# Pairs instead of groups of four in a feed-forward backward, and a changed order of the first loads

## Chip, core and metric

The kernel runs on one core of a Trainium2 chip. The metric is the time of one execution on the device in microseconds (us). Five runs of the kernel before gave 637.66 to 637.92 us, with a median of 637.72 us.

## What is computed

A sequence of 2048 tokens of width 640 goes through two blocks that a gate mixes. All of it is bf16; the kernel returns the output and six gradients.

```python
def _A_ref(x, wqkv, wo):                     # linear attention, 32 heads of 20
    phi = lambda t: jnp.where(t > 0, t + 1, jnp.exp(t)) + 1e-6
    pq, pk = phi(q), phi(k)
    kv = jnp.einsum("bhsd,bhse->bhde", pk, v)
    z = jnp.einsum("bhsd->bhd", pk)
    num = jnp.einsum("bhqd,bhde->bhqe", pq, kv)
    den = jnp.einsum("bhqd,bhd->bhq", pq, z)[..., None] + 1e-6
    ...
def _B_ref(x, w1, w2):                       # feed-forward, 640 -> 1728 -> 640
    h = jnp.maximum(jnp.einsum("bsd,df->bsf", x, w1), 0)
    return jnp.einsum("bsf,fd->bsd", h, w2)

g = sigmoid((x * gate_w).sum(-1, keepdims=True))
out = g * _A_ref(x, A_wqkv, A_wo) + (1 - g) * _B_ref(x, B_w1, B_w2)
# returned: out, and the gradients of x, wqkv, wo, w1, w2, gate_w for a given grad_out
```

## The kernel before

**Tiles and stages.** The tokens are cut into 16 tiles of 128 (`NT`), and the tiles into 4 groups of 4 (`NG`, `G`). The width 640 is 5 chunks of 128 (`KD`); the inner width 1728 is 13 chunks of 128 and a rest of 64, so 14 chunks (`KF`). The stages follow each other on TensorE: the keys of all tiles (`k_part`), the state of the attention (`yp`), queries and forward feed-forward per tile, the gradient of w2, the backward of the attention, **the backward of the feed-forward** (`fb_a`, `fb_b`), the gradient of w1 (`dw1_half`) with the gradient of the keys (`dk_chunk`), the gradients of wqkv, and the gradient of x.

**The start.** `x` and the key weights come in by DMAs that SyncE (SP) and ScalarE (ACT) issue. ACT issues the gate row `gst` (line 408) and then three chunks of the key weights (line 406); SP issues x tiles 0, 1 and 2, weight chunks 3 and 4, and x tiles 3 and 4 (line 334). TensorE needs x transposed. The first `NPE` = 5 tiles are transposed by TensorE itself (`xt`, lines 446 and 449) into PSUM, and DVE and ACT copy them to SBUF (lines 347, 346, 451, 452). The other tiles come transposed by DMA (line 325): one for tiles 5 to 7, one for 8 to 11, one for 12 to 15 (`XLD`). The first of these waits for the matmul `k_part(1, [2])`. The order of TensorE's instructions in this part is written by hand (lines 477 to 502): warm-up matmuls on a constant (line 461) stand before and between the first transposes, and `k_part(i, ks)` adds the products of the weight chunks `ks` to the key tile `kp` of token tile `i`. Behind it, ACT takes an exponential of the finished key tile (line 394) and DVE two steps (396, 397), which also free its PSUM buffer.

**PSUM.** All stages share one tag of four PSUM buffers, each of two banks.

**The backward of the feed-forward.** `fb_a(i, half)` multiplies grad_out with w2 (line 818, 10 matmuls of 2 x 432 columns per half), ACT scales the product (822), DVE applies the mask of the ReLU (824, 825), and behind the second half SP issues a DMA transpose of the tile to a ring of 6 buffers `hTb` (line 325). `fb_b(i)` multiplies the transposed tile with w1, 13 chunks by 26 matmuls (line 341). The rest of 64 rows uses half the rows of the array; `tail_pair` (lines 578 to 583) runs the rests of two tiles side by side, one on rows 0 to 63 (line 582) and one on rows 64 to 127 (line 583). Before the change four tiles form a group: `fb_b` of the two even tiles comes first, then `fb_tails` runs both pairs' rests one behind the other, then the odd tiles. `step(i)` sets what stands between: the two `fb_a` of tile `i`, small products (`small_0` to `small_3`) that use some of the same buffers, and behind tile 15 the first four `dw1_half`. `step` runs four tiles ahead of `fb_b`.

**Order and places.** Outside of the hand-written part a scheduler orders the instructions of each engine. Nearly all of SBUF is one tile, `arena`; a planner (`_Arena.plan`) gives each buffer a place from its size and its planned times, so that buffers with other times can share a place. A load into a place waits for the last reader of what was there.

Of the kernel before, what the change touches and what calls it, by code (L numbers as in the profile page):

```python
# [81 lines left out]
def kernel(  # L82
# [34 lines left out]
    def ring(name, elems, count, t0, t1):  # L117
        ar.add(name, elems * count * B2, t0, t1)
        rings[name] = [elems, count, 0]
# [46 lines left out]
    ar.add("dKVT", KD * D * B2, T_FB + 40, T_FB + 65)  # L166
    ar.add("Q", KD * D * B2, T_FB + 58, T_DWK - 10)
    ar.add("N", KD * D * B2, T_DWK, T_END)
    ring("hTb", KF * P, 6, T_FB, T_DW1 + 5)
    ring("wst", D, 4, T_FB + 88, T_FB + 112)  # L170
    ar.add("dwoT", KD * D * B2, T_FB + 15, T_FB + 52)
    ar.add("dwo", KD * D * B2, T_FB + 45, T_FB + 80)
    ring("dxst", 2 * D, 2, T_FB + 5, T_DW1 + 5)
    ar.add("xN2", NT * D * B2, T_DW1 - 25, T_DX + 5)
    for g in range(NG):
        ar.add(f"xS{g}", G * P * KD * B2, T_DW1, T_DWK - 10)
        ar.add(f"dk{g}", G * D * B2, T_DW1 + 5 + 15 * g, T_DX)
        ar.add(f"dkT{g}", G * D * B2, T_DW1 + 5 + 15 * g, T_END)
    ring("pkr", 2 * D, 3, T_DW1 - 20, T_DWK)
# [31 lines left out]

    xN = aview("xN", NT * DQX, i=NT)
    xN2 = aview("xN2", NT * D, i=NT)
    NPE = 5
    XLD = [(NPE, 2 * G)] + [(g * G, (g + 1) * G) for g in range(2, NG)]

    def xT_view(a, b):
# [109 lines left out]
    def after(late, early, wait=False):  # L327

        tc.add_manual_dep(late.ins, early.ins.name, mybir.DependencyInfo(
            mybir.DependencyClass.Sync if wait else mybir.DependencyClass.NoSync,  # L330
            mybir.DependencyReason.DATA), reason="order of loads")
# [71 lines left out]
        return load_N(xN[:, a:b, 0:D], x2[a * P:b * P, :])  # L403

    def wk_load(eng, k):
        eng.dma_start(wk_s[:, k, 0:D], A_wqkv[k * P:(k + 1) * P, D:2 * D])

    nc.scalar.dma_start(gst[:], gate_w.rearrange("(k p) -> k p", p=P))
    x_load(0, 1)
    wk_load(nc.scalar, 0)  # L410
    x_load(1, 2)
    wk_load(nc.scalar, 1)
    x_load(2, 3)
    wk_load(nc.scalar, 2)
    wk_load(nc.sync, 3)
    wk_load(nc.sync, 4)
    for i in range(3, NPE):
# [19 lines left out]
    def xt(i):  # L437
        if i < 3:
            tp = flat(pp("xtp"))[:, 0:D].rearrange("p (k s) -> p k s", k=KD)
        else:  # L440
            if i == 3:
                kps["x"] = psp.tile([P, 2, 1024], BF16, tag="PP", bufs=4, name="xtp2")
            tp = kps["x"][:, i - 3, 0:D].rearrange("p (k s) -> p k s", k=KD)
        for k in range(KD):
            if i < 3:
                nc.tensor.matmul(tp[:, k, :], lhsT=xN[:, i, csl(k)], rhs=ident[:], start=True, stop=True,
                                 skip_group_check=True)
            else:
                nc.tensor.transpose(tp[:, k, :], xN[:, i, csl(k)], ident[:])
        if i in (1, 2):  # L450
            nc.vector.tensor_copy(xTv[i][0][:, 0:2, :], tp[:, 0:2, :])
            nc.scalar.copy(xTv[i][0][:, 2:KD, :], tp[:, 2:KD, :])
        else:
            copy_out(0 if i == 4 else 1, xTv[i][0], tp)
# [4 lines left out]
    def warm_up(n, cols=512):  # L459
        for _ in range(n):  # L460
            nc.tensor.matmul(wp_[:, 0, 0:cols], lhsT=warm[:, 0:P], rhs=warm[:, 0:cols], start=True, stop=True)

    def k_part(i, ks):
        if 0 in ks:
            kps[i] = pp("kp")
        kp, last = kps[i], 3 if i < 3 else KD - 1
        for k in ks:
            mm = mm_cols(kp, xT(i, k), lambda a, e: wk_s[:, k, a:e], k == 0, k == last, spl=DSP1)
        if last in ks:
            nc.scalar.activation(rg_t[:, i:i + 1], flat(kp)[:, D:D + 1], ACT.Exp, scale=-1.0)  # L470
            phi_chain(flat(kp)[:, 0:D], pkN[:, i, :])
            if i % 4 == 3:
                nc.sync.dma_start(pk_d[(i - 3) * P:(i + 1) * P, :].rearrange("(i p) d -> p i d", p=P),
                                  pkN[:, i - 3:i + 1, :])
        return mm

    wp_ = pp("warm")
    with tc.manual_schedule(engines={mybir.EngineType.PE}):
        warm_up(4)
        warm_up(1, 256)  # L480
        xt(0)
        tp = psp.tile([P, KD, P], BF16, tag="PP", bufs=4, name="gwtp")
        nc.tensor.transpose(tp[:, 0, 0:KD], gst[:], ident[0:KD, 0:KD])
        nc.vector.tensor_copy(wk_s[:, :, D:D + 1], tp[:, 0, 0:KD].unsqueeze(2))
        warm_up(3)
        k_part(0, [0])
        xt(1)
        xt(2)
        k_part(1, [0])
        k_part(0, [1])  # L490
        k_part(1, [1])
        k_part(2, [0, 1])
        k_part(0, [2])
        after(xT_ld[0], k_part(1, [2]), wait=True)
        k_part(2, [2])
        k_part(0, [4, 3])
        xt(3)
        k_part(1, [4, 3])
        xt(4)
        k_part(2, [4, 3])  # L500
        k_part(3, range(KD))
        k_part(4, range(KD))
    for i in range(NT):
        if i >= NPE:
            k_part(i, range(KD))
# [323 lines left out]
            load_T(dhTs[i], hs(i))  # L829

    def fb_b(i):

        if i % 2 == 0:
            ops[i] = pp("dp")
        dp, dT = ops[i], dhTs[i]
        for kf in range(KF - 1):
            mm_cols(dp, dT[:, kf, :], lambda a, e: w1T_s[:, kf, a:e], i % 2 == 0 and kf == 0,
                    i % 2 == 1 and kf == KF - 2)
        if i % 2 == 1:
            fb_out(i)  # L840

    def fb_tails(i):

        for t in (i, i + 2):
            ops[t + 1] = pp("dp")
            tail_pair(ops[t], ops[t + 1], dhTs[t][:, KF - 1, :], dhTs[t + 1][:, KF - 1, :], w1T_s[:, KF - 1, :], True)
        fb_out(i)
        fb_out(i + 2)

    def fb_out(i):  # L850
        pr, ii = i // 2, i % 2
        dhTs.pop(i)
        if ii == 0:
            dx_st[pr] = rnext("dxst").rearrange("p (i d) -> p i d", i=2)
        nc.scalar.copy(dx_st[pr][:, ii, :], flat(ops.pop(i))[:, 0:D])
        if ii == 1:
            nc.scalar.dma_start(rows2(dxB_d, pr), dx_st.pop(pr))

# [19 lines left out]
    def small_3(ts):  # L878
        for t in ts:
            ps = pp("dwv")  # L880
            win_mms(ps, lambda j: YT_s[:, j, csl(t)], dKV_s)
            st = rnext("wst")
            copy_out(t + 1, halves(st), ps[:, :, 0:HD])
            nc.scalar.dma_start(out_2[csl(t), 2 * D:3 * D], st)


# [24 lines left out]
    def dw1_half(n):  # L911
# [8 lines left out]
        nc.scalar.copy(st.rearrange("p (b c) -> p b c", b=2), wp[:, :, 0:NBW])  # L920
        nc.scalar.dma_start(out_4[csl(m), 2 * half * NBW:(2 * half + 2) * NBW], st)

    smalls = {3: small_0, 7: small_2, 12: small_3}

    def step(i):
        if i >= NT:
            dw1_half(i - NT)
            if i == NT:
                for g in range(NG):
                    load_T(xSg[g], x2[g * G * P:(g + 1) * G * P, :])  # L930
                pk_load(0)
                pk_load(1)
            return
        fb_a(i, 0)
        if i in (0, 1):
            dz_add(NT - 2 + i)
        if i == 1:
            for m in range(KD):
                load_T(XT_s[:, :, csl(m)], X_s[:, m, :])
        if i == 2:  # L940
            load_T(woT_s, A_wo)
        if i == 4:
            nc.sync.dma_start(dwoT_d.rearrange("(k p) d -> p k d", p=P), dwoT_s)
        if i == 5:
            load_T(wvT_s, A_wqkv[:, 2 * D:3 * D])
        if i == 6:
            nc.sync.dma_start(dKVT_d.rearrange("(k p) d -> p k d", p=P), dKVT_s)
            load_T(dwo_s, dwoT_d)
        if i == 8:
            nc.sync.dma_start(Q_d.rearrange("(k p) d -> p k d", p=P), Q_s)  # L950
            nc.sync.dma_start(out_3.rearrange("(i p) d -> p i d", p=P), dwo_s)
            nc.sync.dma_start(YT_s, YT_d.rearrange("(k p) d -> p k d", p=P))
        if i == 10:
            load_T(dKV_s, dKVT_d)
        if i in smalls:
            smalls[i](range(0, 2))
        fb_a(i, 1)
        if i in smalls:
            smalls[i](range(2, KD))
        if i == NT - 3:  # L960
            for g in range(NG):
                load_N(xN2[:, g * G:(g + 1) * G, :], x2[g * G * P:(g + 1) * G * P, :])

    for i in range(G):
        step(i)
    for i in range(0, NT, G):
        step(i + G)
        fb_b(i)
        step(i + G + 1)
        fb_b(i + 2)  # L970
        fb_tails(i)
        fb_b(i + 1)
        if i == 0:
            small_1()
        step(i + G + 2)
        fb_b(i + 3)
        step(i + G + 3)
    dk_chunk(0)
    dk_chunk(1)
    done = 2  # L980
    for n in range(G, 2 * KD):
        dw1_half(n)
        while done < NT and done < n * 2 + 1:
            dk_chunk(done)
            done += 1
        if n == 8:
            for g in range(NG):
                load_N(dqN[:, g * G:(g + 1) * G, 0:D], dq_d[g * G * P:(g + 1) * G * P, :])
            nc.vector.tensor_copy(dqN[:, :, D:D + 1], dl_t[:].unsqueeze(2))
# [91 lines left out]
```

## Time and profile before

| what | value |
|---|---|
| median of 5 runs | 637.72 us |
| the profiled execution's own time | 637.66 us |
| its span from first to last instruction | 635.9 us |
| TensorE (PE) matmuls busy | 627.1 us, 99% |
| VectorE (DVE), ScalarE (ACT), GpSimd (POOL) busy | 269.8, 147.7, 97.8 us |
| start of the backward of the feed-forward | 319.48 us |
| first matmul of the gradient of w1 | 429.50 us |
| granted TensorE clock | 1.00 |

The profiled execution lies 0.06 us under the median; 1.8 us of it lie outside of the span. PE is busy nearly all the time, so a change counts if it alters PE's own work or makes PE wait. Matmuls overlap: a row's duration is longer than the distance to the next one, and the distance is what adds up.

### The profile page before, as it was taken

Reading aid. Unit: us, or ns where it says so; the run is one execution under the profiler, and the core shown is the slowest. Engines: PE = TensorE matmul, PEld = TensorE weight load, DVE = VectorE, ACT = ScalarE, POOL = GpSimd, SP = SyncE. Lnnn points to the kernel's source line nnn. Section 1 sums busy time; section 2 is a strip of 40 time slices with the busy share of each in tenths; the row PEclk is TensorE's granted clock in tenths of the full one; section 3 lists DMA queues with packets and bytes.
Section 4 is the critical chain, followed back from the end, with each engine's and each line's share of the span. In section 5 each row is a group of like instructions: output and inputs, shape, how many; then the busy total and the mean of one; then the engine's idle time right before and its main releaser. Section 6 shows DMA issues by size and latency. Waiting matters only on the chain.

```text
span 635.9 us, 10499 instructions
## 1 busy us (share of the span) xinstructions
PE 627.1 (99%) x4406; PEld 352.2 (55%) x4482; DVE 269.8 (42%) x523; ACT 147.7 (23%) x208; POOL 97.8 (15%) x95
## 2 busy tenths in 40 slices
PE   8999999999999999999999999999999999999998
PEld 4555555555555555555555555555555555555554
DVE  4832864454444145555994241510016340004442
ACT  4513321122221123222153343331210011110000
POOL 0050742453334022322001000000000000000000
PEclk9999999999999999999999999999999999999999
DMA  7999996544554793942799998955137659991111
GB/s 177 315 395 206 192 248 148 121 92 84 129 120 97 194 198 100 211 135 73 168 190 219 260 256 178 240 136 126 49 117 180 172 109 230 242 258 42 42 42 43
DMA packets 228473, 103.93 MB, mean 163 GB/s; under 512 B 185098, under 2 KB 227722, under 8 KB 228426
## 3 DMA queue, kind: packets, MB, share of 16 engines
q1 hardware_dynamic: 217344, 90.48, 60.9%
q10 hardware_dynamic: 11082, 12.79, 6.2%
q8 instruction: 35, 0.57, 0.4%
q14 instruction: 12, 0.10, 0.0%
HBM read 28.43 MB, written 28.84 MB: 90 GB/s over the span
## 4 chain that ended last, share of the span: by engine, by line
PE 98%; issue 1%; ACT 1%; DVE 0%
PE op L341 12%; PE dxp L341 10%; PE hp L565 9%; PE gp L818 9%; PE w1p L917 9%; PE dp L341 9%; PE w2p L341 9%; PE yp L341 3%; PE xp L341 3%; PE rp L341 3%; PE wkp L341 3%; PE dkp L341 3%; PE qp L341 3%; PE kp L341 3%; PE wqp L1014 3%; PE wqp L1015 1%
## 5 line engine op out<-in xcount | busy, mean ns | idle before, releaser
L341 PEld LDWEIGHTS <-arena 128*128 128x128 bf16 x2978 | 230.6, 98 | 179.6 <-issue 2.1
L341 PE MATMUL op<-arena 128*128 128x128 bf16 (+1 forms) x567 | 79.1, 298 | 0.5
L565 PE MATMUL hp<-arena 128*128 128x432 bf16 x320 | 62.6, 346 | 0.0
L341 PE MATMUL dxp<-arena 128*128 128x128 bf16 (+1 forms) x441 | 60.8, 297 | 0.5
L818 PE MATMUL gp<-arena 128*128 128x432 bf16 x320 | 60.9, 346 | 0.2
L917 PE MATMUL w1p<-arena 128*128 128x432 bf16 x320 | 60.0, 346 | 0.0
L341 PE MATMUL dp<-arena 128*128 128x128 bf16 (+1 forms) x402 | 58.3, 296 | 0.9
L341 PE MATMUL w2p<-arena 128*128 128x128 bf16 (+1 forms) x408 | 58.5, 297 | 0.4
L917 PEld LDWEIGHTS <-arena 128*128 128x128 bf16 x320 | 30.9, 98 | 26.6
L818 PEld LDWEIGHTS <-arena 128*128 128x128 bf16 x320 | 30.7, 98 | 26.2 <-issue 0.5
L565 PEld LDWEIGHTS <-arena 128*128 128x128 bf16 x320 | 30.0, 98 | 26.7 <-issue 1.8
L822 ACT ACTIVATE tb<-gp,omg_t 128x864 bf16<-128x864 f32 x32 | 31.4, 980 | 40.9 <-PE gp L818 39.2
L825 DVE TENSOR_TENSOR arena<-tb,tb 128x864 bf16<-128x864 bf16 x32 | 19.4, 606 | 48.8 <-ACT tb L822 48.2
L901 DVE TENSOR_TENSOR tb<-dkp,dzb 128x640 bf16<-128x640 f32 x16 | 13.1, 820 | 59.2 <-PE dkp L341 59.2
L604 DVE SCALAR_TENSOR_TENSOR tb<-op,arena 128x640 bf16<-128x640 f32 x16 | 13.1, 821 | 47.7 <-ACT arena L602 47.7
L528 POOL TENSOR_TENSOR f<-tb,zb 128x640 f32<-128x640 bf16 x16 | 23.3, 1457 | 60.4 <-DVE tb L397 49.6
L711 POOL TENSOR_TENSOR f<-zb,grd 128x640 f32<-128x640 bf16 x16 | 20.3, 1270 | 75.2 <-DVE grd L709 75.2
L602 ACT CAST arena<-op 128x640 bf16<-128x640 f32 x16 | 11.1, 692 | 81.8 <-PE op L341 47.2
L1038 DVE TENSOR_TENSOR arena<-dxp,f 128x640 bf16<-128x640 f32 x15 | 12.4, 825 | 36.7 <-PE dxp L341 36.7
L920 ACT CAST arena<-w1p 128x864 bf16<-128x864 f32 x10 | 8.8, 878 | 75.2 <-PE w1p L917 75.2
L542 POOL TENSOR_TENSOR arena<-tb,grd 128x640 bf16<-128x640 bf16 x16 | 20.3, 1269 | 30.0 <-DVE grd L536 23.5
L341 PE MATMUL rp<-arena 128*128 128x128 bf16 (+1 forms) x157 | 24.2, 297 | 0.2
(121 smaller groups left out, 609.5 us busy)
## 6 DMA issues: line engine op xcount, KB each, us to landing
out_dram<-arena ACTq DMA_DIRECT2D x28, 160.0 KB, 3.7
arena<-in_A_x_dram SPq DMA_DIRECT2D x6, 640.0 KB, 5.1
pk_d<-arena SPq DMA_DIRECT2D x4, 640.0 KB, 9.7
arena<-in_grad_out_dram SPq DMA_DIRECT2D x4, 640.0 KB, 4.6
e_d<-arena SPq DMA_DIRECT2D x8, 320.0 KB, 2.8
out_dram<-arena ACTq DMA_DIRECT2D x8, 320.0 KB, 2.3
arena<-e_d SPq DMA_DIRECT2D x8, 320.0 KB, 3.6
dq_d<-arena SPq DMA_DIRECT2D x8, 320.0 KB, 3.5
```

Of the source, the lines that this page charges most:

```text
L341: mm = nc.tensor.matmul(ps_tile[:, b, 0:e - a], lhsT=lhsT, rhs=rhs_fn(a, e), start=start, stop=stop, **kw)
L528: return nc.gpsimd.tensor_tensor(tzs[i][:], pqs[i][:], zb[:], ALU.mult)
L542: nc.gpsimd.tensor_tensor(heads(pg), heads(pq[:]), hb(grd[:]), ALU.mult)
L565: nc.tensor.matmul(hp[:, nb, 0:NBW], lhsT=xT(i, k), rhs=w1_s[:, k, blk * NBW:(blk + 1) * NBW], start=(k == 0), stop=(k == KD - 1))
L604: nc.vector.scalar_tensor_tensor(jk[:], flat(op)[:, 0:D], 1.0, doX(i)[:, 0:D], ALU.mult, ALU.mult, accum_out=T_t[:, i:i + 1])
L711: nc.gpsimd.tensor_tensor(heads(wz[:]), heads(zb[:]), hb(w32[:]), ALU.mult)
L818: nc.tensor.matmul(gp[:, nb, 0:NBW], lhsT=doTg[i // G][:, k, gsl(i)], rhs=w2T_s[:, k, blk * NBW:(blk + 1) * NBW], start=(k == 0), stop=(k ...
L822: nc.scalar.activation(gs[:], gp[:, :, 0:NBW], ACT.Copy, scale=omg_t[:, i:i + 1])
L825: nc.vector.tensor_tensor(hs(i)[:, rng], msk[:], gs[:].rearrange("p b c -> p (b c)"), ALU.mult)
L901: nc.vector.tensor_tensor(a_[:], flat(kp)[:, 0:D], dzb[:], ALU.add)
L917: nc.tensor.matmul(wp[:, nb, 0:NBW], lhsT=xN2[:, i, csl(m)], rhs=hs(i)[:, blk * NBW:(blk + 1) * NBW], start=(i == 0), stop=(i == NT - 1))
L1014: nc.tensor.matmul(wp[:, 0, :], lhsT=lhsT, rhs=dqN[:, i, 0:512], start=(i == 0), stop=(i == NT - 1))
```

## The change

There are two parts.

At the start, the first chunk of the key weights is issued ahead of the gate row on ACT, and one of three warm-up matmuls behind the first transpose goes; the gate row's transpose moves behind the other two. `NPE` falls from 5 to 4: x tile 4 is neither loaded for TensorE's transpose nor transposed by it, and the first DMA transpose brings tiles 4 to 7. It waits for `k_part(0, [1])`, which stands five key steps earlier than `k_part(1, [2])`.

In the backward of the feed-forward, the groups of four become pairs: `tail_pair` runs once per pair, directly behind `fb_b` of its even tile. `fb_a` still runs four tiles ahead (`LAGB`); the halves of `fb_a` stand both ahead of `fb_b` for even tiles and on its two sides for odd ones. The ring `hTb` has 5 buffers, the transposed x for `dk_chunk` (`xS`) is planned 25 us earlier and its loads stand ahead of the last tile, and `small_3` copies with ACT alone where it took turns with DVE. The planner gives most buffers another place.

```diff
-    ring("hTb", KF * P, 6, T_FB, T_DW1 + 5)
+    ring("hTb", KF * P, 5, T_FB, T_DW1 + 5)
...
-        ar.add(f"xS{g}", G * P * KD * B2, T_DW1, T_DWK - 10)
+        ar.add(f"xS{g}", G * P * KD * B2, T_DW1 - 25, T_DWK - 10)
...
-    NPE = 5
+    NPE = 4
...
-    nc.scalar.dma_start(gst[:], gate_w.rearrange("(k p) -> k p", p=P))
     x_load(0, 1)
-    wk_load(nc.scalar, 0)
+    gst_ld = nc.scalar.dma_start(gst[:], gate_w.rearrange("(k p) -> k p", p=P))
+    after(gst_ld, wk_load(nc.scalar, 0))
     x_load(1, 2)
-    wk_load(nc.scalar, 1)
+    after(wk_load(nc.scalar, 1), gst_ld)
...
         xt(0)
+        warm_up(2)
         tp = psp.tile([P, KD, P], BF16, tag="PP", bufs=4, name="gwtp")
         nc.tensor.transpose(tp[:, 0, 0:KD], gst[:], ident[0:KD, 0:KD])
         nc.vector.tensor_copy(wk_s[:, :, D:D + 1], tp[:, 0, 0:KD].unsqueeze(2))
-        warm_up(3)
         k_part(0, [0])
         xt(1)
         xt(2)
         k_part(1, [0])
-        k_part(0, [1])
+        after(xT_ld[0], k_part(0, [1]), wait=True)
         k_part(1, [1])
         k_part(2, [0, 1])
         k_part(0, [2])
-        after(xT_ld[0], k_part(1, [2]), wait=True)
+        k_part(1, [2])
         k_part(2, [2])
         k_part(0, [4, 3])
         xt(3)
         k_part(1, [4, 3])
-        xt(4)
         k_part(2, [4, 3])
         k_part(3, range(KD))
-        k_part(4, range(KD))
...
     def fb_b(i):
-
-        if i % 2 == 0:
+        pr, ii = i // 2, i % 2
+        dT = dhTs.pop(i)
+        if ii == 0:
             ops[i] = pp("dp")
-        dp, dT = ops[i], dhTs[i]
+        dp = ops.pop(i)
         for kf in range(KF - 1):
...
         if ii == 0:
+            ops[i + 1] = pp("dp")
+            tail_pair(dp, ops[i + 1], dT[:, KF - 1, :], dhTs[i + 1][:, KF - 1, :], w1T_s[:, KF - 1, :], True)
             dx_st[pr] = rnext("dxst").rearrange("p (i d) -> p i d", i=2)
-        nc.scalar.copy(dx_st[pr][:, ii, :], flat(ops.pop(i))[:, 0:D])
+        nc.scalar.copy(dx_st[pr][:, ii, :], flat(dp)[:, 0:D])
...
-            copy_out(t + 1, halves(st), ps[:, :, 0:HD])
+            nc.scalar.copy(halves(st), ps[:, :, 0:HD])
...
-    for i in range(0, NT, G):
-        step(i + G)
-        fb_b(i)
-        step(i + G + 1)
-        fb_b(i + 2)
-        fb_tails(i)
-        fb_b(i + 1)
-        if i == 0:
-            small_1()
-        step(i + G + 2)
-        fb_b(i + 3)
-        step(i + G + 3)
+    for i in range(NT + LAGB):
+        if i < NT:
+            fb_a(i, 0)
...
+            if i % 2 == 0 or i == NT - 1:
+                fb_a(i, 1)
+        else:
             dw1_half(i - NT)
+        if i >= LAGB:
+            fb_b(i - LAGB)
+        if i < NT - 1 and i % 2 == 1:
+            fb_a(i, 1)
...
+        if i == NT - 2:
+            for g in range(NG):
+                load_T(xSg[g], x2[g * G * P:(g + 1) * G * P, :])
+            pk_load(0)
+            pk_load(1)
```

More of the change, by code (lines that the diff above doesn't have):

```diff
@@ L405, in wk_load @@
     def wk_load(eng, k):
-        eng.dma_start(wk_s[:, k, 0:D], A_wqkv[k * P:(k + 1) * P, D:2 * D])
-    nc.scalar.dma_start(gst[:], gate_w.rearrange("(k p) -> k p", p=P))
+        return eng.dma_start(wk_s[:, k, 0:D], A_wqkv[k * P:(k + 1) * P, D:2 * D])
     x_load(0, 1)
-    wk_load(nc.scalar, 0)
+    gst_ld = nc.scalar.dma_start(gst[:], gate_w.rearrange("(k p) -> k p", p=P))
+    after(gst_ld, wk_load(nc.scalar, 0))
     x_load(1, 2)
-    wk_load(nc.scalar, 1)
+    after(wk_load(nc.scalar, 1), gst_ld)
     x_load(2, 3)
-    wk_load(nc.scalar, 2)
+    after(wk_load(nc.scalar, 2), gst_ld)
     wk_load(nc.sync, 3)
@@ L831, in fb_b @@
     def fb_b(i):
-        if i % 2 == 0:
+        pr, ii = i // 2, i % 2
+        dT = dhTs.pop(i)
+        if ii == 0:
             ops[i] = pp("dp")
-        dp, dT = ops[i], dhTs[i]
+        dp = ops.pop(i)
         for kf in range(KF - 1):
[L837 to L852, printed above, removed]
+            mm_cols(dp, dT[:, kf, :], lambda a, e: w1T_s[:, kf, a:e], ii == 0 and kf == 0, ii == 1 and kf == KF - 2)
         if ii == 0:
+            ops[i + 1] = pp("dp")
+            tail_pair(dp, ops[i + 1], dT[:, KF - 1, :], dhTs[i + 1][:, KF - 1, :], w1T_s[:, KF - 1, :], True)
             dx_st[pr] = rnext("dxst").rearrange("p (i d) -> p i d", i=2)
-        nc.scalar.copy(dx_st[pr][:, ii, :], flat(ops.pop(i))[:, 0:D])
+        nc.scalar.copy(dx_st[pr][:, ii, :], flat(dp)[:, 0:D])
         if ii == 1:
@@ L921, in dw1_half @@
         nc.scalar.dma_start(out_4[csl(m), 2 * half * NBW:(2 * half + 2) * NBW], st)
+    LAGB = 4
     smalls = {3: small_0, 7: small_2, 12: small_3}
-    def step(i):
-        if i >= NT:
-            dw1_half(i - NT)
[L928 to L943, printed above, removed]
-        if i == 5:
[L945 to L957, printed above, removed]
@@ new lines @@
+    for i in range(NT + LAGB):
+        if i < NT:
+            fb_a(i, 0)
+            if i in (0, 1):
+                dz_add(NT - 2 + i)
+            if i == 1:
+                for m in range(KD):
+                    load_T(XT_s[:, :, csl(m)], X_s[:, m, :])
+            if i == 2:
+                load_T(woT_s, A_wo)
+            if i == 5:
+                load_T(wvT_s, A_wqkv[:, 2 * D:3 * D])
+            if i == 4:
+                nc.sync.dma_start(dwoT_d.rearrange("(k p) d -> p k d", p=P), dwoT_s)
+            if i == 6:
+                nc.sync.dma_start(dKVT_d.rearrange("(k p) d -> p k d", p=P), dKVT_s)
+                load_T(dwo_s, dwoT_d)
+            if i == 8:
+                nc.sync.dma_start(Q_d.rearrange("(k p) d -> p k d", p=P), Q_s)
+                nc.sync.dma_start(out_3.rearrange("(i p) d -> p i d", p=P), dwo_s)
+                nc.sync.dma_start(YT_s, YT_d.rearrange("(k p) d -> p k d", p=P))
+            if i == 10:
+                load_T(dKV_s, dKVT_d)
+            if i in smalls:
+                smalls[i](range(0, 2))
+            if i % 2 == 0 or i == NT - 1:
+                fb_a(i, 1)
+        else:
+            dw1_half(i - NT)
+        if i >= LAGB:
+            fb_b(i - LAGB)
+        if i < NT - 1 and i % 2 == 1:
+            fb_a(i, 1)
+        if i == 5:
+            small_1()
@@ L962, in step @@
                 load_N(xN2[:, g * G:(g + 1) * G, :], x2[g * G * P:(g + 1) * G * P, :])
-    for i in range(G):
-        step(i)
-    for i in range(0, NT, G):
-        step(i + G)
-        fb_b(i)
-        step(i + G + 1)
-        fb_b(i + 2)
-        fb_tails(i)
-        fb_b(i + 1)
-        if i == 0:
-            small_1()
-        step(i + G + 2)
-        fb_b(i + 3)
-        step(i + G + 3)
+        if i == NT - 2:
[3 more added lines that the diff above has]
+            pk_load(1)
     dk_chunk(0)
@@ L980 @@
     done = 2
-    for n in range(G, 2 * KD):
+    for n in range(LAGB, 2 * KD):
         dw1_half(n)
```

## The prediction

> **What bounds the kernel now.** I read the page first: its busy times, then the list of what PE waited for, then PE's timeline in the two places that the change touches. Engine, busy time, share of the span:
>
> ```profile
> PE 627.1 (99%) x4406; PEld 352.2 (55%) x4482; DVE 269.8 (42%) x523; ACT 147.7 (23%) x208; POOL 97.8 (15%) x95
> ```
>
> PE has no idle time to give back except a few tenths. The list of its waits (who, for whom, us in total) has three lines:
>
> ```profile
> PE warm L461 <- DVE arena L401: 1.3, 1, 1.3
> PE kp L341 <- DVE arena L451: 0.2, 1, 0.2
> PE kp L341 <- DVE arena L397: 0.2, 1, 0.2
> ```
>
> All are in the first 12 us. So in the backward stage only PE's own steps and new waits count, and at the start the chain to the first keys. The chain of waits at the start (start, us, what):
>
> ```profile
> 5.40 0.53 PE kp L341 x2
> 5.93 0.50 PE xtp L446 x5
> 6.43 0.02 issue
> 6.46 0.44 DVE arena L451
> 6.89 0.05 issue
> 6.94 2.91 PE kp L341 x20
> ...
> 10.05 0.60 ACT tb L394
> ...
> 11.04 0.84 DVE arena L397
> ```
>
> The reader sees that PE goes on at 6.94 when DVE has copied x tile 1, and that tile 3's keys (11.92) wait for the PSUM buffer of tile 0's, through ACT and DVE. The PE timeline around one group of rests (start, us, line, output, shape):
>
> ```profile
> 350.08 0.22 PE L341 MATMUL dp<-arena 128*128 128x128 bf16 x1
> 350.23 0.39 PE L582 MATMUL dp<-arena 64*128 64x512 bf16 x1
> ...
> 350.73 0.22 PE L582 MATMUL dp<-arena 64*128 64x128 bf16 x1
> ...
> 350.88 0.39 PE L341 MATMUL dp<-arena 128*128 128x512 bf16 x1
> ```
>
> Two pairs' rests run here in one piece. Entering it takes 0.15 us from start to start, leaving it 0.15, where a 128-column step between full-array matmuls takes 0.055 (five on line 449 take 0.44 with the last one's 0.22).
>
> Last, DMA transposes of x, each alone in its window of the DMA view; the last number is us from issue to landing:
>
> ```profile
> arena<-in_A_x_dram SPq DMA_TRANSPOSE x1, 4.8
> arena<-in_A_x_dram SPq DMA_TRANSPOSE x1, 7.1
> arena<-in_A_x_dram SPq DMA_TRANSPOSE x1, 5.5
> ```
>
> They are tiles 5 to 7 (issued 9.05), tiles 8 to 11 behind it (10.72), and four tiles on an empty queue (410.34).
>
> **The backward stage.** The matmuls are the same in number and shape: 13 chunks per tile, four half-row matmuls per pair. What changes is how often PE goes into half rows and back. One piece costs 2 x (0.15 - 0.055) = 0.19 us. Before there are 4 such pieces, after 8: **+0.76 us**. The forward pass has the pair form already: at 98.02 to 98.55 the same two distances of 0.15 stand around one pair, so the price does not depend on the group's length. PE is the bound on both sides of each piece, so nothing hides it.
>
> *Buffers.* With pairs at most two `dp` buffers are held, with the group of four up to four. The stage shows no PE wait for `dp` before, so nothing is won. Three waits of 0.29 stand where the small products end (335.43, 368.17, 403.16): three of them take 1.1 us of PE and the next tile needs a buffer that ACT empties in 0.98 after its own 0.2 delay. The first two stay as they are. At the third, ACT now takes all copies: behind the pair's rests it empties `dp` (0.69) and then the products (0.69 each). The last product waits for the first of these (free about 1.0 after the rests, PE there at 0.85: 0.15), the next `gp` for the second (free 1.7, PE there at 1.57: 0.13). Sum 0.28 against 0.29: **0**, between -0.2 (the old turns) and +0.7 (one more copy in the row).
>
> *Transposed tiles.* A tile's transpose is issued behind ACT and DVE (0.98 + 0.61 + 0.18) and lands 4 to 7 us later. The rests of a pair need the odd tile six `gp` blocks of 1.83 and two `fb_b` of 3.5 after it was made, 18 us; before it was four blocks and two `fb_b`, 14 us. A slot of the ring of 5 is free when `fb_b` of the tile five earlier is done, which is behind. The x loads for the keys' gradient now stand between these transposes on SP and hold it 3.5 us each (410.34: 3.48); SP's longest issue here, 8.5 us at 361.57, still fits in 18 - 2 - 7 = 9. **0**; without that cover a late tile costs what exceeds 9 us.
>
> *Places.* Loads wait for other readers now. The closest case I find is the transpose of w1's last chunk, which now stands ahead of the last forward transpose on SP: it issues in 1.3 us, where that tile landed 2.9 us ahead of its use. **0**, up to +0.3.
>
> **The start.** One warm-up less is 0.43 us of PE at half speed (4.76 to 5.19). The first key matmul then waits for DVE's copy of x tile 0 (3.93 + 0.82 = 4.75), and starts at about 4.85 instead of 5.19; with the gate row's transpose now in line, 0.29 of this is left at the next transposes, and DVE's copy and the step at 6.94 move by the same **-0.29**. Against it: x tile 0 is issued at 0.80 and lands at 2.90, just in time for 3.15; weight chunk 0 now is issued at the same moment, not 0.6 later. Its 160 KB take 0.47 us at the 340 GB/s that the DMAs move there (3 to 7 us), so tile 0 lands 0 to 0.47 later, of which 0.1 is free. That gives -0.29 to +0.08; I take half sharing, **-0.1**. The gate row stands behind the chunk, which needs no more than the 3.3 us it took before: it is there at 4.2, needed at 4.6. The earlier first chunk itself gives nothing: it landed at 4.65 and was used at 5.19.
>
> Matmul distances double before about 6.2 us (0.107 against 0.056 for 128 columns), 4.95 us after the first matmul at 1.25. The Trainium skill (TensorE: Matmul & The Clock Gate, "What's actually happening") gives about 3.4 us of sustained work and a free-running window, and says that the moment varies; five runs within 0.26 us speak against a large variation here. By its rule a gap within the window could move the opening to the next window, and half of 3.4 us would be lost: the sum would be +2.4 instead of +0.7. It speaks against the change; no row shows such a miss.
>
> *Tile 4.* Let K be the step at 6.94. Before, tile 5 starts at 14.66 = K + 7.71. PE loses the two parts of `xt(4)`, 0.28 of matmuls and a wait of 0.20 for DVE's copy of tile 3, and tile 3's keys take the transposes' buffer, free when that copy is done, so the wait at 11.92 goes too: tile 4 could start at K + 5.47, 0.88 earlier than before. But now it needs the DMA. That is issued when `k_part(0, [1])` ends, K + 0.74, and tile 4 starts about 0.14 after landing. With a landing time L the start changes by the larger of -0.88 and L - 5.47. No row shows four tiles at this place. Three tiles took 4.8 there (-0.7); four tiles on an empty queue 5.5; four behind another transfer 7.1 (+1.6). The queue is empty here (x tile 3 landed 7.5), and 4.8 and one more 160 KB at some 210 GB/s give 5.5 too. I take 5.5: **0**. All that was won is spent on waiting. The second transpose, needed 5.5 us later, has about 1 us to spare.
>
> **Sum.** +0.76 + 0 + 0 + 0 - 0.1 + 0 = +0.66. On the profiled 637.66 that is 638.3; the median lies 0.06 higher, so **638.4**. Ends: -0.29 - 0.7 + 0.76 - 0.2 = -0.4 (637.3), and +0.08 + 1.6 + 0.76 + 0.3 = +2.7 (640.4).
>
> **Rivals.**
>
> 1. *Tile 4 is there in time* (L under 4.8, as three tiles took). For: fewer bytes are under way at 7.4 than at 9.05. Against: one tile more. The start gives -0.8, the sum is -0.05: 637.7. Chance 0.15.
> 2. *Slower: the first DMA transpose is late.* Place: `k_part(4)`. Price L - 5.47; it decides from L = 6.1 on, where the sum passes +1.28. For: SP sends the next two transposes directly behind, and x's four tiles took 6.3 at 398 and 7.1 at 10.72. Against: both stood behind other transfers. With L = 6.6: 639.5. Chance 0.2.
> 3. *The switches are cheaper than the rows show, or the group's buffers held something up that the waits don't name*: 637.0 and under. Against: PE's distances are complete in this stage. Chance 0.05.
>
> **Numbers.** The forecast (638.0 to 638.9) has 0.6. I call 0.2%, 1.28 us, the bound, about what a measurement of this kernel can tell from no change. Forecast and rival 1 lie within: 0.75. Rival 2 is slower: 0.21 with the late gate. Faster by over 0.2% needs rival 3 and a start at its low end: 0.04. The range 637.3 to 639.8 leaves out less than 2 in 10.
>
> **What would show it.** In the profile after: eight places in the backward stage with 0.15 in and out of half rows; PE's waits name one long wait, on line 341 for the DMA of x, 0.8 to 0.9 us at about 12.3; the step at 6.94 lies at 6.7 to 6.9; the last dwv waits are two of 0.1 to 0.2. I am wrong if PE waits for a transposed tile or a load between 319 and 470 us, if matmuls are still 0.107 apart after 6.6 us, or if tile 4's wait is under 0.2 or over 1.5 us.

## The result, and the profile after

| | before | after |
|---|---|---|
| median | 637.67 us (45 runs) | 638.41 us (25 runs) |
| lowest to highest | 636.85 to 639.55 | 638.04 to 639.17 |
| ratio after / before | | 1.0014, 95% interval 1.0009 to 1.0019 |
| the profiled execution, its span | 637.66, 635.9 | 638.19, 636.5 |

The change costs 0.74 us, a little over a thousandth, and the forecast was 638.4. The busy line of the changed kernel (engine, us, share of the span, instructions):

```profile
PE 627.1 (99%) x4399; PEld 351.0 (55%) x4476; DVE 267.3 (42%) x520; ACT 149.3 (23%) x210; POOL 97.8 (15%) x95
```

PE's busy time has not moved. It is counted with overlaps and cannot show a few tenths, so the waits and the distances have to. Its whole list of waits (who, for whom, us in total, times, longest):

```profile
PE warm L461 <- DVE arena L401: 1.3, 1, 1.3
PE kp L341 <- DMA arena<-in_A_x_dram: 0.4, 1, 0.4
PE xtp L446 <- DMA arena<-in_A_x_dram: 0.3, 1, 0.3
PE kp L341 <- DVE arena L451: 0.2, 1, 0.2
```

Two of the lines are new and both name the DMA of x: tile 4's keys, as forecast, and the transposes of tile 0, which was not. The wait for DVE's line 397 is gone, as forecast. No line belongs to the backward stage. The chain of waits at the start of the changed kernel (start, us, what):

```profile
0.80 2.84 DMA arena<-in_A_x_dram
...
3.69 0.72 PE xtp L446 x5
4.41 0.85 PE warm L461 x2
5.26 0.12 PE gwtp L484
5.37 0.67 PE kp L341 x2
...
6.86 0.75 PE kp L341 x5
7.61 5.24 DMA arena<-in_A_x_dram
...
12.90 3.12 PE kp L341 x21
```

Tile 0's transposes start at 3.69, where it was 3.15. The step that was at 6.94 is at 6.86 all the same. At 7.61 PE finishes the step that the DMA transpose waits for, 5.24 us pass until the transpose has landed, and 0.05 later tile 4 starts, at 12.90. Before it started at 13.29.

The PE timeline of the changed kernel around the first pair's rests (start, us, line, output, shape):

```profile
342.67 0.39 PE L580 MATMUL dp<-arena 64*128 64x512 bf16 x1
342.68 0.39 PE L581 MATMUL dp<-arena 64*128 64x512 bf16 x1
342.90 0.22 PE L580 MATMUL dp<-arena 64*128 64x128 bf16 x1
342.90 0.22 PE L581 MATMUL dp<-arena 64*128 64x128 bf16 x1
343.05 0.36 PE L816 MATMUL gp<-arena 128*128 128x432 bf16 x1
```

One pair alone, with the last full-array matmul at 342.52: 0.15 into the half rows, 0.15 out of them. Eight such places stand between 342 and 459 us.

To see where the time went, the start of the same instruction is compared between the two traces. From about 20 us on, such differences stay equal to 0.01 us for hundreds of us. In the two timelines the backward of the feed-forward begins, and behind it the first `dkp` block, at these times. Before:

```profile
319.31 2.90 PE L818 MATMUL gp<-arena 128*128 128x432 bf16 x15
...
467.58 2.88 PE L341 MATMUL dkp<-arena 128*128 128x512 bf16 x19
```

After:

```profile
318.94 3.27 PE L816 MATMUL gp<-arena 128*128 128x432 bf16 x17
...
468.03 2.88 PE L341 MATMUL dkp<-arena 128*128 128x512 bf16 x20
```

So the changed kernel is 0.38 ahead at 319 us (0.37 from the rounded lines) and 0.45 behind at 468: the stage between takes **0.83 us** more, and the start of this one execution 0.38 less. Whether the 0.38 belongs to the kernel or to this execution is what the experiments had to tell.

### The profile page after: what moved, and what is told of

It reads as the page before. It is cut to its first block, busy times and chain, and to the rows that moved or that the text cites. A ratio compares the mean times of both kernels' runs of the same rounds, so it can differ in the third digit from the quotient of the medians.

```text
span 636.5 us, 10487 instructions
## 1 busy us (share of the span) xinstructions
PE 627.1 (99%) x4399; PEld 351.0 (55%) x4476; DVE 267.3 (42%) x520; ACT 149.3 (23%) x210; POOL 97.8 (15%) x95
## 4 chain that ended last, share of the span: by engine, by line
PE 97%; DMA 1%; issue 1%; ACT 0%; DVE 0%
PE op L341 12%; PE dxp L341 10%; PE gp L816 9%; PE hp L563 9%; PE w1p L903 9%; PE w2p L341 9%; PE dp L341 9%; PE yp L341 3%; PE xp L341 3%; PE wkp L341 3%; PE rp L341 3%; PE dkp L341 3%; PE qp L341 3%; PE kp L341 3%; PE wqp L992 3%; DMA arena<-in_A_x_dram 1%
## 5 line engine op out<-in xcount | busy, mean ns | idle before, releaser
L341 PE MATMUL dp<-arena 128*128 128x512 bf16 (+1 forms) x400 | 58.0, 296 | 0.8
L1016 DVE TENSOR_TENSOR arena<-dxp,f 128x640 bf16<-128x640 f32 x15 | 12.4, 825 | 36.7 <-PE dxp L341 36.7
```

The lines of the kernel that those rows point to most:

```text
L341: mm = nc.tensor.matmul(ps_tile[:, b, 0:e - a], lhsT=lhsT, rhs=rhs_fn(a, e), start=start, stop=stop, **kw)
```

## The experiments

The theory to begin with: eight pieces of half rows in place of four cost the backward stage 0.76 to 0.83, and the start gives 0.1 to 0.4 back. The rivals: the start gives nothing (A), the pieces cost less and something else of the new order the rest (B).

**Only the pairs.** The changed kernel with the whole old start:

```
-    NPE = 4
+    NPE = 5
...
(loads and PE's order of the start as in the kernel before)
```

> The kernel before with only the feed-forward backward in pairs; its start is the old one. Theory (the difference is a sum: eight pieces of half rows in place of four cost 4 x 0.19 = 0.76 us, the new start gives back 0.38): 0.76 over the kernel before, about 638.4, and all of it between 340 and 460 us. Rival A (the new start gives nothing in the median, what the trace shows of it is lost later): 0.7 over, the same as the changed kernel. Rival B (the pieces cost about 0.4 and something else of the new order costs the rest): 0.4 from the pieces in the PE timeline, and the rest at PE waits that the changed kernel also has.

Measured: 638.57 against 637.71, ratio 1.0014 (1.0005 to 1.0022). In the trace the stage takes 0.83 more than before, exactly what the changed kernel shows, and there is no new wait in it. Rival B falls: it needs new waits, and pieces at half the price, which the run with twice as many pieces below excludes. The ratio is that of the whole change, which is what rival A expects of the median.

**Only the new start**, with groups of four. It was run twice, on different chips:

```
-    NPE = 5
+    NPE = 4
...
(loads and PE's order of the start as in the changed kernel)
```

> The kernel before with only the new start (weight chunk 0 ahead of the gate row, two warm-ups in place of three, tiles 4 to 7 by one DMA transpose); groups of four as before. Theory: 0.38 under the kernel before, about 637.3; x tile 0 lands near 3.6, the DMA transpose of tiles 4 to 7 takes 5.2 to 5.3, PE waits for it 0.4 to 0.6, and tile 4 starts near 12.9. Rival A (what the start gives is lost later): 0 in the median, 637.7. Rival C (the early start varies from run to run, a DMA transpose over 6 us in some): 637.7 and more, with a spread over 1 us.

> The same kernel as the start alone, on one chip with the run above, for the part of the spread that is no property of a kernel: its first profile had the clock open at 9.05 us and was 0.86 behind the kernel before at 15 us. Theory (the opening falls between 4.8 and 9 us at a moment that differs from run to run, and the order of the loads and the earlier tile 4 take from each other): an opening at another moment than 9.05, and a median within 0.4 of the kernel before, whatever this profile shows. Rival (this start opens the clock late by its own gap): an opening after 7 us again, and a median 0.5 or more over the kernel before.

Measured: 638.18 against 637.71, ratio 1.0003 (0.9994 to 1.0012), and 638.00 against 637.70, ratio 1.0006 (0.9997 to 1.0015). The expected gain of 0.38 is not there. The first profile of this kernel is 0.86 *behind* the kernel before from 15 us on, with the same instructions at the start with which the changed kernel was 0.38 ahead. Its PE timeline shows why:

```profile
4.33 1.06 PE L461 MATMUL warm<-arena 128*128 128x512 bf16 x2
...
5.97 1.27 PE L446 MATMUL xtp<-ident,arena 128*128 128x128 bf16 x10
7.22 3.17 PE L341 MATMUL kp<-arena 128*128 128x512 bf16 x15
```

Ten transposes take 1.27 us here, 0.107 from start to start: PE is still at half speed. In the single rows behind, distances are 0.427 for 512 columns until 8.80 and 0.216 from 9.20 on. I call the moment at which the distances halve the opening of PE's clock. Here it is at about 9.05, in the changed kernel's profile at 6.0. (The granted clock is listed as 1.00 in both; only the distances tell.) The second profile of this kernel has the opening at about 7.1, the changed kernel with split rests, whose start is also the same, at 7.3. So there are four executions of one start:

| execution | clock opens | transpose issued, took | tile 4 starts | against before at 319 us |
|---|---|---|---|---|
| changed kernel | 6.0 | 7.61, 5.24 | 12.90 | -0.38 |
| start alone, again | 7.1 | 7.87, 5.69 | 13.61 | +0.32 |
| split rests | 7.3 | 7.95, 5.78 | 13.78 | +0.50 |
| start alone | 9.05 | 8.51, 5.59 | 14.14 | +0.86 |

The later the clock opens, the later the transpose is issued and tile 4 starts. It isn't the clock alone: of the 0.71 between the first two rows at tile 4, 0.26 come from the issue and 0.45 from a transpose that took longer. The profile after was the luckiest of the four. In medians the start gives nothing that could be told: rival A is right, though not for the reason it named. The repetition was to part chance from a late opening that belongs to this start. Its median, 0.30 over the kernel before, is within the 0.4 of the theory and under the 0.5 of the rival; its opening, again at about 7, fits both.

**Tile 4 back on PE**, the rest of the new start kept:

```
-    NPE = 4
+    NPE = 5
...
         k_part(1, [4, 3])
+        xt(4)
         k_part(2, [4, 3])
         k_part(3, range(KD))
+        k_part(4, range(KD))
```

The DMA transpose, of tiles 5 to 7, waits for `k_part(1, [2])` again.

> The new start, but tile 4 is transposed by PE as before and the DMA transpose takes tiles 5 to 7 and waits where it waited before; groups of four as before. Theory (of the 0.38 only 0.08 comes from the order of loads and the warm-up, 0.30 from tile 4): 0.08 under the kernel before, about 637.6; the step that was at 6.94 lies at 6.86, tile 5 starts at 14.58. Rival D (tile 4 is worth nothing, the clock that opens 0.2 earlier is worth it all): 637.3, tile 5 at 14.3.

Measured: 638.00 against 637.71, ratio 1.0004 (0.9995 to 1.0013). It is slower than both the theory and rival D named, and does not part them. In its profile the clock opens at about 4.5, earlier than in any other: the two warm-ups behind tile 0's transposes take 0.37 and 0.31 to the next instruction, where they take 0.43 and 0.57 in the changed kernel. The step at 6.94 is 0.36 ahead. At 20 us only 0.09 of it is left: tile 8's keys start 0.26 late behind the second DMA transpose, which landed at 18.59 (17.85 before). The profile of the kernel with only the pairs did the same: it was 0.40 ahead at this step, lost 0.53 to a transpose that landed at 18.82, and was 0.14 behind at 20 us. So these two show an early clock spent on the next transfer, and not what tile 4 is worth.

**Twice as many pieces.** The changed kernel with the rests of each pair in two places:

```
         for kf in range(KF - 1):
-            mm_cols(dp, dT[:, kf, :], ...)
+            for b, (a, e) in enumerate(DSPL):
+                nc.tensor.matmul(dp[:, b, 0:e - a], ...)
+                if ii == 0 and kf == KF - 2:
+                    tail_bank(dp, ops[i + 1], ..., b)
...
-            tail_pair(dp, ops[i + 1], ...)
```

> The changed kernel, with the half-row matmuls of each pair in two places: those of the first 512 columns ahead of the last full chunk's 128 columns, those of the 128 columns behind it. Same matmuls, 16 pieces in place of 8. Theory (each entry into half rows and each return costs 0.095 whatever stands between): 8 x 0.19 = 1.52 over... that is, 1.52 for eight pieces more, of 0.19 each: 1.5 over the changed kernel, about 639.9, with sixteen places of 0.15 in and 0.15 out. Rival E (what costs is the return into a full-array matmul that reads other weights, or a piece of one pair of matmuls drains in the shadow of the next): under 0.8 over the changed kernel.

Measured: 640.77 against 637.71, ratio 1.0043 (1.0030 to 1.0055). The stage takes 1.70 us more than in the changed kernel, in eight steps of 0.21. Its PE timeline at the first pair:

```profile
343.49 0.39 PE L585 MATMUL dp<-arena 64*128 64x512 bf16 x1
343.50 0.39 PE L586 MATMUL dp<-arena 64*128 64x512 bf16 x1
343.82 0.23 PE L844 MATMUL dp<-arena 128*128 128x128 bf16 x1
343.98 0.23 PE L585 MATMUL dp<-arena 64*128 64x128 bf16 x1
343.98 0.23 PE L586 MATMUL dp<-arena 64*128 64x128 bf16 x1
344.14 0.36 PE L821 MATMUL gp<-arena 128*128 128x432 bf16 x1
```

The lone full matmul at 343.82 stands 0.32 behind the 512-column pair (0.216 without a switch) and 0.16 ahead of the next half rows (0.056): both ways are paid again. Rival E falls. A piece costs 1.70 / 8 = 0.21.

**A gap in PE's work before x tile 0**, filled in the new start, and opened in the kernel before:

```
(new start)             (kernel before)
-        warm_up(4)     -        warm_up(4)
+        warm_up(5)     -        warm_up(1, 256)
                        +        warm_up(2)
```

> The new start with groups of four, and one more 512-column warm-up ahead of x tile 0's transposes, so that TensorE has work where it waited 0.5 to 0.7 us for x tile 0 (3.15 to 3.8). In the six profiles so far the matmul distances change from 0.107 to 0.056 at 4.8, 5.4, 6.0, 6.25, 7.3 and 9.05 us, and every difference between kernels before 319 us is made in the first 15 us. Theory G (the clock opens later when there is a gap in the first 4 us): the opening lies before 7 us, the median comes down to 637.5 or less, the spread is under 1.5 us. Rival H (the opening falls at a moment of its own in each run, gap or not): the median stays at 638 within 0.3, and the spread at over 2 us.

> The kernel before, with two 512-column warm-ups at the start in place of four and a half, so that TensorE has nothing to do from 2.1 to about 3.15 us; nothing else is changed, and x tile 0 is transposed when it was. Theory G (a gap delays the opening): opening after 6.6 us, the median 0.5 to 1.5 above the kernel before. Rival H: the same median within 0.3.

Measured: filled, 637.85 against 637.78, ratio 1.0002 (0.9994 to 1.0011), opening at 5.65, lowest to highest 0.9 us apart. With a gap, 638.49 against 637.78, ratio 1.0014 (1.0005 to 1.0023). Filled, theory G has the opening and the spread right, and rival H the median. With the gap, theory G came true on both counts. The ten transposes of x tiles 1 and 2 in the kernel before:

```profile
5.73 0.97 PE L446 MATMUL xtp<-ident,arena 128*128 128x128 bf16 x10
```

And in the kernel with the gap, with the keys behind them:

```profile
6.12 1.27 PE L446 MATMUL xtp<-ident,arena 128*128 128x128 bf16 x10
7.38 3.30 PE L341 MATMUL kp<-arena 128*128 128x512 bf16 x20
```

With the gap all ten are 0.107 apart, the first two key steps behind 7.38 still take 0.40 and 0.39 for 512 columns, and the distance is 0.216 from 8.33 on. The clock opened at about 8.2, 2.0 later than the 6.25 of the kernel before, and the median rose by 0.71. Of the 0.84 that this profile is behind, 0.40 arises in these two key steps at half speed. The other 0.44 is there at the first key matmul already, which waited for weight chunk 0 (landed at 5.59, 4.65 before; x tile 1 at 5.38, 4.48 before); whether the gap has to do with that, no run shows.

Over all twelve profiles, the five without a gap ahead of tile 0's transposes opened at 5.35 to 6.8. Of the seven with one, four opened at about 7 or later (7.1, 7.3, 8.2, 9.05) and three at 4.5 to 6.0. This fits a gap that lets the clock open late, but not always; one or two profiles of a kernel are too few to show it. (The 4.8 in the first expectation is the run with tile 4 on PE, whose rows give 4.5.)

**The gate row first again**, in the new start with groups of four:

```
-    x_load(0, 1)
-    gst_ld = nc.scalar.dma_start(gst[:], ...)
-    after(gst_ld, wk_load(nc.scalar, 0))
+    nc.scalar.dma_start(gst[:], ...)
+    x_load(0, 1)
+    wk_load(nc.scalar, 0)
```

> The new start with groups of four, but the loads in the old order (gate row, x tile 0, weight chunk 0). Theory (weight chunk 0, issued at the same moment as x tile 0, is what delays that tile by 0.7): x tile 0 lands at 2.9 to 3.1, weight chunk 0 at 4.5 to 4.7, the first key matmul starts near 4.9 in place of 5.33 to 5.46, and the kernel is 0.2 to 0.4 under the new start in the old groups. Rival (the delay of x tile 0 is hidden by the wait for DVE's copy and the gate row): the same time within 0.2.

Measured: 637.21 against 637.78, ratio 0.9992 (0.9984 to 1.0001); x tile 0 lands at 3.06, weight chunk 0 at 4.39, and the first key matmul starts at 4.80. This is 0.6 under the kernel before, with an interval that just takes in no change, where the new start with the chunk ahead stood 0.3 to 0.5 over it. The delay of x tile 0 is a cost of the order of loads and it isn't hidden: the theory holds, with a larger gain than the 0.2 to 0.4 it named. How much of the gain is the tile and how much the clock is not parted: with the tile there at 3.06 the gap ahead of its transposes is gone too, and the clock opened at 5.35.

**The DMA transpose of tiles 4 to 7 earlier**, in the new start with groups of four:

```
-        k_part(0, [0])
+        after(xT_ld[0], k_part(0, [0]), wait=True)
...
-        after(xT_ld[0], k_part(0, [1]), wait=True)
+        k_part(0, [1])
```

> The new start with groups of four, and the DMA transpose of tiles 4 to 7 issued when the first chunk of tile 0's keys ends (near 5.9 us) in place of that of its second chunk (7.6 to 8.5). Theory (what tile 4 waits for is the landing, 5.2 to 5.8 us behind the issue): it lands near 11.5, PE does not wait on line 341 for x, tile 4 starts 0.5 earlier, time 0.5 under the new start in the old groups. Rival (the transposes share the DMAs with the last loads, which land until 7.9): it takes over 7 us, or x tile 3 and weight chunks 3 and 4 land later and PE waits for them: no gain.

Measured: 637.39 against 637.78, ratio 0.9997 (0.9988 to 1.0006). The transpose is issued at 5.96 and takes 6.02, longer than 5.24 but not the over 7 of the rival, lands at 11.98, and tile 4 starts at 12.19 with no wait. PE's waits in this profile:

```profile
PE warm L461 <- DVE arena L401: 1.3, 1, 1.3
PE xtp L446 <- DMA arena<-in_A_x_dram: 0.4, 1, 0.4
PE kp L341 <- DVE arena L451: 0.2, 1, 0.2
```

The line for tile 4 is gone. In the profile the start is 1.10 ahead of the kernel before; the median gains 0.4 and its interval takes in no change.

**Both of these edits together**, with groups of four:

> Groups of four as before; the new start with both of the last edits: the gate row ahead of weight chunk 0, and the DMA transpose of tiles 4 to 7 behind the first chunk of tile 0's keys. Theory (the two gains add, since one makes the chain to the step at 6.94 shorter and the other takes tile 4's wait away): the step near 6.45, the transpose issued near 5.7 and landed by 11.8, tile 4 at 11.9 to 12.1, 1.2 to 1.4 ahead of the kernel before; median 636.3 to 636.6, below both kernels. Rival (issued among the loads the transpose takes 6.5 and more, or the loads become late for it): tile 4 at 12.4 or later, 637 and over.

Measured: 636.72 against 637.70, ratio 0.9989 (0.9980 to 0.9998). That is faster than both kernels, by 1.0 us over the one before, 0.1 us over the end of the expected range. The transpose, seen alone in its window of the DMA view (the last number is us from issue to landing):

```profile
arena<-in_A_x_dram SPq DMA_TRANSPOSE x1, 6.1
```

It was issued at 5.72 and landed at 11.84, and tile 4 did not wait. But the step at 6.94 lies at 7.05 and not at 6.45, since x tile 2 landed only at 6.72 in this execution and PE waited 0.5 us for it. So tile 4 started at 12.51, which is the rival's "12.4 or later", and this profile is 0.78 ahead of the kernel before and not 1.2 to 1.4:

```profile
6.76 0.45 PE L446 MATMUL xtp<-ident,arena 128*128 128x128 bf16 x5 [0.54 <-DMA arena<-in_A_x_dram]
```

## Why the prediction was right, point by point

- **The backward stage, +0.76: the mechanism as predicted, the size 0.07 to 0.09 small.** A piece costs 0.21 where I had 0.19. I counted the two distances of 0.15. The first wide matmul behind each switch also takes longer to the next one, 0.226 where 512 columns take 0.216 elsewhere and 0.193 where 432 take 0.183: 0.02 per piece. Four pieces are 0.85.
- **Buffers, 0: right.** The first two waits of 0.29 are unchanged. At the third there are waits of 0.20 and 0.07, 0.27 in all for 0.28 predicted. 0.85 less 0.02 is the stage's 0.83.
- **Transposed tiles and places, 0: right.** PE waits for no transposed tile and no load between 319 and 470 us.
- **The start up to the step at 6.94, -0.1: wrong in its parts.** The step that failed is the bound "tile 0 lands 0 to 0.47 later". It lands 0.74 later, 3.64 for 2.90. In all seven profiles with weight chunk 0 issued at the same moment it landed at 3.64 to 3.77, in the five with the gate row first at 2.90 to 3.08. The chunk's bytes at the full rate, 0.47, were no upper end. The profile's -0.08 came with a clock that opened 0.25 earlier than before; in the three other executions of this start the step is at +0.18 to +0.28.
- **The clock.** I took "five runs within 0.26 us" as evidence against a varying opening. The 45 runs of that kernel spread over 2.7 us, so five so close together were chance. In twelve profiles the opening lies between 4.5 and 9.05 us, 3.3 to 7.8 after the first matmul at 1.25, and the differences between executions of one start arise ahead of 20 us, all but a wait of 0.13 at 67 us in the one with only the pairs. The Trainium skill (TensorE: Matmul & The Clock Gate, "What's actually happening") calls the window free-running and the moment run-variable. The runs agree with the second, and I weighed it too low; its spread of 0.5 us each way is smaller than the 1.5 each way that one and the same start showed here (6.0 to 9.05). I priced a late opening at 1.7 us; the four executions of this start lie at most 1.24 apart (-0.38 to +0.86), of which the transpose's own length is a part.
- **Tile 4, 0: the mechanism right.** The predicted wait on line 341 is there, and the start follows the landing: with L = 5.24 tile 4 gains 0.23 by the rule L - 5.47, and 0.09 more because it starts 0.05 behind the landing and not 0.14. The taken L of 5.5 lies within the 5.24 to 5.86 of six executions that issue at this place. The wait itself was listed as 0.41 and not 0.8 to 0.9, for the same two reasons and because the list counts from the modelled end of the last matmul, 0.16 after the next could start. Where tile 4 did not wait, in the run with the transpose earlier, it started 5.46 behind the step at 6.94 (6.73 to 12.19), for the 5.47 of the prediction. Of the two ends, 4.8 never came, so rival 1 fell, and 6.1 came only where the transpose was issued among the loads, and there it did no harm. Rival 2 fell for the median.
- **The sum.** 0.83 and a start between -0.1 (changed kernel: 0.74 - 0.83) and +0.5 (the start alone), none of which the intervals can tell from 0. I had 0.76 - 0.1. The total is right because the main term stands in distances that repeat to 0.01 us, and because the small errors went opposite ways; the start's -0.1 is not confirmed.

What stays open: whether it was the gap in PE's work that delayed the clock's opening where it came late, and how much of the runs' spread is the opening and how much the landing of x tiles 1 and 2, which also varied (3.98 to 5.38 and 4.95 to 6.72).

## What to carry to other kernels

Count how often PE goes between full-array and half-row matmuls, and take the price from one round trip in the trace, the slower first matmul behind each switch included; grouping such matmuls pays in proportion. A start that is read from a single profile isn't a property of the kernel: compare the same instruction across several executions of the same code before believing tenths in the first 20 us. When a transfer is started by a step of the engine that will wait for it, move that step earlier rather than make the engine faster, and keep other transfers from being issued beside the one that comes due first.

## What the runs showed of the hardware that was not expected

- PE's clock opened between 3.3 and 7.8 us after its first matmul at 1.25 us. In four executions whose starts held the same instructions it opened at 6.0, 7.1, 7.3 and 9.05 us, while the granted clock was listed as 1.00.
- Leaving out three of the warm-up matmuls on a constant, so that PE had a gap ahead of x tile 0, cost 0.71 us in the median; in its profile the clock opened at 8.2 and not at 6.25.
- A 160 KB load issued at the same moment on another queue delayed x tile 0 by 0.6 to 0.9 us, and not by the 0.47 that its bytes take at the 340 GB/s moved a little later.
- The DMA transpose of four tiles took 5.24 to 5.86 us when issued at 7.2 to 8.5, and 6.02 and 6.12 when issued among the last loads, at 5.96 and 5.72.
- One round trip between full array and half rows cost PE 0.21 us, the same for a piece of two matmuls as for one of eight.
